# Quad 1 prepared inside the prologue, global scores in two column tiles, and top-k steps moved by one quad

## The chip, the cores and the metric

The kernel runs on one core of one Trainium2 chip. The core has a matrix engine (TensorE, PE in the profile), a vector engine (VectorE, DVE), an activation engine (ScalarE, ACT), GpSimd (POOL), and SyncE (SP), which here only issues transfers. The metric is the device time of one execution in microseconds. The kernel before takes 274.02 us, the median of three runs (272.31 to 275.62). Its profiled execution has a span of 268.8 us, and every moment named below is counted from the start of that span.

## The reference

Two stages follow one another: an attention with local and global tokens, and a layer of experts in which each expert takes at most 80 tokens.

```python
# attention: batch 8, heads 8, 512 local and 32 global tokens, head_dim 64
k_all = concat([k_g, k_l]); v_all = concat([v_g, v_l])
out_g = softmax(scale * q_g @ k_all.T) @ v_all          # global queries see every key
s_ll = where(|i - j| <= 32, scale * q_l @ k_l.T, -1e9)  # local queries: a band of keys
s_l  = concat([scale * q_l @ k_g.T, s_ll])              # ... and all global keys
out_l = softmax(s_l) @ concat([v_g, v_l])
x = concat([out_g, out_l]) as (4352 tokens, 512)

# experts: 8, w1 512x1024, w2 1024x512, capacity 80
logits = x @ w_gate; e = argmax(logits); gate = softmax(logits)[e]
for each expert: keep the 80 tokens with the largest gate
    out[tok] = gate * (relu(x[tok] @ w1[e]) @ w2[e])     # all other rows are 0
```

## The kernel before

A *quad* is four heads of one batch entry; there are 16 quads, numbered q. For each, queries and keys are loaded (`load_qk`), cast to fp16 and regrouped (`regroup`, into `qkr`), transposed on TensorE into `qkT` (`T_chunk`), and copied on GpSimd into a second arrangement (`kO_copy`, `kt_copy`). `L_fill` makes the local scores, `G_fill` the scores of local queries against global keys, `Q_fill` those of global queries. ScalarE takes the exponential of each out of PSUM. `G_all`, `H_chunk` and `Q_chunk` multiply by the values, `X_chunk` transposes the result for the gate logits. The steps `La` to `Ld` do the routing of one batch entry, two quads later; `some(n)` runs n pieces of the top-k work of a group of batch entries.

The global keys and queries stand in block-diagonal tiles, zeroed once:

```python
qbd = apool.tile([P, B, 4, 64], FP16, name="qbd")
kbd = apool.tile([P, B, 2, 320], FP16, name="kbd")
nc.gpsimd.memset(kbd[:], 0.0)
nc.gpsimd.memset(qbd[:], 0.0)

def G_fill(q):
    g_ps = psS([P, 512], FP32, f"G_ps{q}")          # pool "S": two PSUM buffers
    for j in range(2):
        nc.tensor.matmul(out=g_ps[:], lhsT=kbd[:, b, qd, 128 * j:128 * j + 128],
                         rhs=qkT[q % 2][:, j, 0:512], start=(j == 0), stop=(j == 1))
    nc.scalar.activation(out=s["eG"][:], in_=g_ps[:], func=AF.Exp, scale=scale)

def Q_fill(q, j):
    gq_ps = psS([P, NB, 64], FP32, f"gq_ps{q}_{j}")
    # ... five matmuls 128x64 with qbd, then the exponential

def L_fill(q, j):
    l_ps = [psS([P, 512], FP32, f"l_ps{q}_{j}_{hh}") for hh in range(2)]
    # ... one matmul of bandneg, 16 of 64x64, then two exponentials
```

The prologue and the first steps (cut):

```python
load_v(0)                      # v of quad 0, and vg of batch entry 0 in one transfer
load_qk(1)
regroup(0, 0)
regroup(0, 1, nc.vector.tensor_copy, nc.scalar.copy)
# ...
warm0(9)                       # matmuls that only keep TensorE busy
T_chunk(0, 0)
T_chunk(0, 1, (nc.vector.tensor_copy, nc.scalar.copy))
kO_copy(0, 0); kO_copy(0, 1); kt_copy(0)
setup_globals(0, 1, 1)         # fills kbd of batch entry 0
warm0(3)
# ... band
shift_v(0); L_fill(0, 0); mask(0, 0)
warm0(2)
setup_globals(0, 1, 0)         # fills qbd
L_fill(0, 1)
warm0(2)
G_fill(0)
for j in range(2):
    Q_fill(0, j)
regroup(1, 0, nc.vector.tensor_copy); mask(0, 1); regroup(1, 1, nc.vector.tensor_copy)
# ... loads
nc.gpsimd.memset(zt, 0.0); nc.gpsimd.memset(fin[:], 0.0)
for q in range(NQ):            # first = (q == 0)
    if late is not None and q == NQ - 1:
        Lc(late); some(2)
    G_all(q); H_chunk(q, 0)
    if first: T_chunk(1, 0)
    Q_chunk(q)
    if first: regroup(2, 0, ...); T_chunk(1, 1); kO_copy(1); kt_copy(1)
    elif q + 2 < NQ: T_chunk(q + 2, 0)
    if not first and q + 1 < NQ: L_fill(q + 1, 0); mask(q + 1, 0)
    # ... La, regroup(q + 3, 0), shift_v(q + 1)
    some(NS[q][0]); H_chunk(q, 1)
    if first: regroup(2, 1, ...); load_qk(4); L_fill(1, 0); mask(1, 0); shift_v(1)
    # ... Lb1
    some(NS[q][1])
    # ... L_fill(q + 1, 1), T_chunk(q + 2, 1), kO_copy, kt_copy when not first
    H_chunk(q, 2)
    # ... mask(q + 1, 1), Lm, Lb2; for the first: L_fill(1, 1), mask(1, 1), T_chunk(2, 0)
    G_fill(q + 1); Q_fill(q + 1, 0)
    H_chunk(q, 3)
    # ... for the first: T_chunk(2, 1), kO_copy(2), kt_copy(2)
    X_chunk(q, 0); Q_fill(q + 1, 1)
    # ... Lb3
    C_chunk(q); X_chunk(q, 1)
    some(NS[q][2])
```

`NS[14]` is `[1, 2, 1]`. After the loop come the rest of the routing, the zeroing of the output (17 transfers from `zt`), the global top-k, the gather of the kept tokens, eight experts and the scatter.

Of the kernel before, what the change touches and what calls it, by code (L numbers as in the profile page):

```python
# [18 lines left out]
P = 128  # L19
# [60 lines left out]
def kernel(  # L80
# [128 lines left out]
    def load_v(q):  # L209
# [6 lines left out]
        if qd == 0:  # L216
            nc.sync.dma_start(out=vg[b % 2][:, :, 0:64], in_=v_g[b].rearrange("(q f) g d -> (f g) q d", f=4))
# [11 lines left out]
    regroup(0, 0)  # L229
    regroup(0, 1, nc.vector.tensor_copy, nc.scalar.copy)  # L230
    load_qk(2)
    load_v(1)
    misc = const("misc", FP32)

# [22 lines left out]
    nc.vector.tensor_copy(out=identbf[:], in_=ident16[:])  # L257
# [7 lines left out]

    kbd = apool.tile([P, B, 2, 320], FP16, name="kbd")
    nc.gpsimd.memset(kbd[:], 0.0)
    nc.gpsimd.memset(qbd[:], 0.0)

    def setup_globals(b0, b1, *ts):  # L270
        for t, bd in ((1, kbd), (0, qbd)):
# [9 lines left out]
            for x, y, r, f in parts:  # L281
                if t == 1:
                    dst = kbd[x, b0:b1, r.start // 2, :].rearrange("x b (r c) -> x b r c", r=2)[
                        :, :, :, 64 * f:64 * f + 32]
                else:
                    dst = qbd[x, b0:b1, r, 32 * f:32 * f + 32]
                nc.vector.tensor_copy(out=dst, in_=src[y, :, :, f, :])
# [8 lines left out]
    for i in range(2):  # L296
        nc.vector.memset(Ls[i][:], 0.0)
    sc_all = cpool.tile([P, B, NB, E], FP32, name="sc_all")
# [32 lines left out]
    def G_fill(q):  # L331
# [4 lines left out]
        for j in range(2):  # L336
            nc.tensor.matmul(out=g_ps[:], lhsT=kbd[:, b, qd, 128 * j:128 * j + 128],  # L337
                             rhs=qkT[q % 2][:, j, 0:512], start=(j == 0), stop=(j == 1))
        nc.scalar.activation(out=s["eG"][:], in_=g_ps[:], func=AF.Exp, scale=scale)

    def Q_fill(q, j):
        b, qd = divmod(q, 2)
        gq_ps = psS([P, NB, 64], FP32, f"gq_ps{q}_{j}")
        for u in range(NB):
            k = qkT[q % 2][:, j, 512 + 128 * u:640 + 128 * u] if u < 4 else kbd[:, b, qd, 128 * j:128 * j + 128]
# [5 lines left out]
    def L_fill(q, j):  # L351
# [9 lines left out]
        for t in range(8) if q else (1, 2, 3, 4, 5, 6, 7, 0):  # L361
# [31 lines left out]
    def G_all(q):  # L393
# [5 lines left out]
        for u in range(4):  # L399
            for h in range(4):  # L400
                nc.tensor.matmul(out=s["o"][h][:, u, :],  # L401
                                 lhsT=s["eG"][32 * h:32 * h + 32, 128 * u:128 * u + 128],
                                 rhs=vg[b % 2][32 * h:32 * h + 32, qd, :], start=(u == 0), stop=False,
                                 skip_group_check=True)
# [21 lines left out]
    def Q_chunk(q):  # L426
# [4 lines left out]
        for u in range(NB):  # L431
            for h in range(4):
                f = slice(32 * (h // 2), 32 * (h // 2) + 32)
                x = slice(32 * h, 32 * h + 32)
                eQ = s["eQ"][h % 2]
                nc.tensor.matmul(out=og[x, :], lhsT=eQ[:, u, f] if u < 4 else eQ[x, u, f],  # L436
# [552 lines left out]
```

## Time and profile before

| what | value |
|---|---|
| time, median of 3 runs | 274.02 us (272.31 to 275.62) |
| span of the profiled execution | 268.8 us |
| TensorE busy | 230.1 us, 86% of the span |
| VectorE, ScalarE, GpSimd busy | 146.0, 136.6, 166.7 us |
| mean granted TensorE clock | 0.958 |
| first matmul of a quad's turn (G_all) of quads 0, 1, 2 | 15.14, 29.77, 40.60 us |
| the same of quads 14 and 15 | about 175.1, 187.6 us |
| first gather of tokens, first scatter | 228.31, 250.88 us |

"Busy" is the time in which an engine has an instruction in work. A releaser, written behind an arrow, is what ended the idle time before an instruction. The granted clock is the share of full TensorE speed in a stretch. The line numbers (L401) are those of the kernel before. The chain of work that ended last gives 42% of the span to TensorE, 19% to transfers and 15% to VectorE.

### The profile page before, as it was taken

The numbers are of one execution on the slowest core, as the hardware profiler recorded it, in microseconds if no ns is written. First come the engines' busy times: TensorE is split into PE (matmuls) and PEld (weight loads), VectorE is DVE, ScalarE is ACT, GpSimd is POOL, SyncE is SP. The second block draws the span as 40 slices with busy tenths as digits, with TensorE's granted clock in tenths as the row PEclk, the third lists the DMA queues.
The fourth block names the chain that finished last, engine by engine and source line by source line (L and its number), as shares of the span: only waits on it lengthen the run. The fifth ranks groups of instructions, "written<-read, shape, count | busy, mean of one in ns | idle before, by whom it ended". The sixth has DMA issues, their size and how long they took to land.

```text
span 268.8 us, 9537 instructions
## 1 busy us (share of the span) xinstructions
PE 230.1 (86%) x4022; PEld 159.4 (59%) x4022; DVE 146.0 (54%) x452; ACT 136.6 (51%) x237; POOL 166.7 (62%) x231
## 2 busy tenths in 40 slices
PE   6886979998899999998799999897986999399980
PEld 2365756776677577675657667665733445187750
DVE  2661661723753557776455955769687976012220
ACT  4455386776856759576486956835050000024420
POOL 9637776858859677784856878698362000790532
PEclk9798999999999999999999999999797999979995
DMA  7999879999999899899599969986999999999971
GB/s 231 303 278 202 265 134 222 196 221 193 241 218 248 169 220 255 162 265 264 130 230 235 234 116 184 183 151 126 182 296 262 235 233 307 408 413 239 214 221 50
DMA packets 67355, 60.05 MB, mean 223 GB/s; under 512 B 45808, under 2 KB 50160, under 8 KB 67312
## 3 DMA queue, kind: packets, MB, share of 16 engines
q1 hardware_dynamic: 59328, 40.61, 58.9%
q0 software_dynamic: 7840, 18.80, 37.7%
q8 instruction: 31, 0.51, 0.8%
q14 instruction: 12, 0.10, 0.1%
q10 hardware_dynamic: 144, 0.03, 0.1%
HBM read 61.57 MB, written 14.70 MB: 284 GB/s over the span
## 4 chain that ended last, share of the span: by engine, by line
PE 42%; DMA 19%; DVE 15%; issue 9%; ACT 7%; POOL 4%; SPq 1%; POOLq 1%; ACTq 0%; DVEq 0%
DMA out_dram<-zt 11%; PE o_ps L414 9%; DMA x_scr<-xgb 6%; PE o_ps L401 6%; PE T_ps L310 5%; PE og L436 5%; DVE xn L422 4%; ACT qkT L318 4%; PE x_ps L451 4%; PE lt_ps L473 3%; DVE scT L580 3%; PE l_ps L368 2%; DMA vb<-in_v_l_dram 2%; PE G_ps L337 2%; DVE lst L578 2%
## 5 line engine op out<-in xcount | busy, mean ns | idle before, releaser
L381 POOL TENSOR_TENSOR eL<-eL,band 128x512 f32<-128x512 f32 x30 | 37.9, 1265 | 34.6 <-ACT eL L373 34.6
L318 ACT COPY qkT<-T_ps 128x1024 f16<-128x1024 f16 x31 | 31.5, 1017 | 37.4 <-PE T_ps L310 37.4
L414 PE MATMUL o_ps<-vb,eL 128*64 128x65 f32 x1024 | 44.4, 230 | 0.0
L373 ACT ACTIVATE eL<-l_ps 128x512 f32<-128x512 f32 x64 | 34.8, 598 | 15.0 <-PE l_ps L368 14.8
L414 PEld LDWEIGHTS o_ps<-vb,eL 128*64 128x64 f32 x1024 | 35.7, 139 | 9.9 <-issue 6.0
L162 ACT CAST qkr<-qkb 128x1024 f16<-128x1024 f32 (+1 forms) x26 | 27.1, 1047 | 2.4 <-DMA qkb<-in_q_l_dram 2.0
L451 PE MATMUL x_ps<-misc,xn 128*128 128x128 f32 x128 | 20.5, 283 | 7.6 <-DVE xn L422 7.0
L649 PE MATMUL w_ps<-w1sb,onesb 128*128 128x512 bf16 x110 | 26.8, 398 | 0.0
L327 POOL COPY kO<-qkT 128x512 f16<-128x512 f16 x31 | 19.4, 650 | 11.0 <-ACT qkT L318 4.7
L927 ACT ACTIVATE fhT<-h_ps 128x320 bf16<-128x320 f32 x16 | 6.7, 431 | 36.4 <-PE h_ps L925 36.4
L903 POOL DMA_INDIRECT xg<-x_scr,idx x8 | 7.8, 971 | 27.2 <-DMA out_dram<-zt 25.0
L422 DVE TENSOR_TENSOR xn<-o_ps,rec 128x512 f32<-128x512 f32 x32 | 22.1, 692 | 2.4 <-POOL eL L381 0.5
L310 PE MATMUL T_ps<-ident,qkr 128*128 128x128 f16 x256 | 20.8, 227 | 2.8 <-DVE qkr L162 1.5
L421 DVE RECIPROCAL rec<-o_ps 128x8 f32<-128x8 f32 x32 | 6.5, 204 | 28.9 <-PE o_ps L414 28.7
L451 PEld LDWEIGHTS x_ps<-misc,xn 128*128 128x128 f32 x128 | 13.4, 140 | 10.2 <-PE gq_ps L346 6.3
L462 POOL CAST xb<-xn 128x1024 bf16<-128x1024 f32 x16 | 16.6, 1036 | 4.6 <-DVE xn L422 4.6
L649 PEld LDWEIGHTS <-onesb 128*128 128x128 bf16 x110 | 10.7, 102 | 13.9 <-issue 3.5
L310 PEld LDWEIGHTS <-qkr 128*128 128x128 f16 x256 | 15.2, 101 | 5.7 <-DVE qkr L162 1.6
L401 PE MATMUL o_ps<-vg,eG 32*128 32x65 f32 x512 | 18.4, 280 | 0.0
L441 DVE RECIPROCAL rg<-og 128x1 f32<-128x1 f32 x16 | 2.7, 169 | 28.1 <-PE og L436 28.1
L223 POOL COPY vb<-vb 64x1040 f32<-64x1040 f32 x16 | 17.1, 1067 | 0.9
L401 PEld LDWEIGHTS o_ps<-vg,eG 32*128 32x128 f32 x512 | 16.1, 190 | 2.3 <-issue 1.7
(156 smaller groups left out, 473.6 us busy)
## 6 DMA issues: line engine op xcount, KB each, us to landing
out_dram<-zt SPq DMA_DIRECT2D x17, 512.0 KB, 13.4
qkb<-in_q_l_dram SPq DMA_DIRECT2D x16, 512.0 KB, 5.2
qkb<-in_k_l_dram SPq DMA_DIRECT2D x16, 512.0 KB, 7.2
vb<-in_v_l_dram SPq DMA_DIRECT2D x16, 384.0 KB, 9.4
w2sb<-in_moe_w_dram POOLq DMA_DIRECT2D x12, 512.0 KB, 9.0
w1sb<-in_moe_w_dram POOLq DMA_DIRECT2D x10, 512.0 KB, 10.1
x_scr<-xb SPq DMA_DIRECT2D x8, 514.0 KB, 8.8
vb<-in_moe_w_dram POOLq DMA_DIRECT2D x6, 512.0 KB, 12.3
```

Of the source, the lines that this page charges most:

```text
L162: cp(out=qkr[q][:, t, i].rearrange("p i g d -> p g i d"), in_=qkb[q % 2][:, t, :, i])
L223: nc.gpsimd.tensor_copy(out=v[64:128, 17:33], in_=v[64:128, 0:16])
L310: nc.tensor.transpose(out=T_ps[:, i].rearrange("x a p -> x (a p)"), in_=qkr[q][:, t, i].rearrange("p g d -> p (g d)"), identity=ident16[:, :])
L318: nc.scalar.copy(out=dst, in_=src)
L327: (nc.gpsimd if q or a else nc.vector).tensor_copy(out=kO[q % 2][:, a], in_=qkT[q % 2][:, a, 576:1088].rearrange("x (u w y) -> x u w y", w ...
L373: nc.scalar.activation(out=eL[:], in_=l_ps[hh][:], func=AF.Exp, scale=scale)
L381: eng.tensor_tensor(out=eL[:], in0=eL[:], in1=band[:].rearrange("p t i -> p (t i)"), op=ALU.mult)
L401: nc.tensor.matmul(out=s["o"][h][:, u, :], lhsT=s["eG"][32 * h:32 * h + 32, 128 * u:128 * u + 128], rhs=vg[b % 2][32 * h:32 * h + 32, qd, ...
L414: nc.tensor.matmul(out=o[64 * odd:64 * odd + 64, u, :], lhsT=s["eL"][h][:, 64 * t:64 * t + 64], rhs=v[:, 17 * odd + 4 * h + u, :], start=F ...
L422: nc.vector.tensor_tensor(out=s["xn"][:, :, 64 * h - 64:64 * h + 64].rearrange("p u (h d) -> p h u d", h=2), in0=o2[:, :, :, 0:64], in1=re ...
L451: nc.tensor.transpose(out=x_ps[:, 128 * u:128 * u + 128], in_=s["xn"][:, u, 128 * j:128 * j + 128], identity=identf[:, :])
L649: nc.tensor.matmul(out=w_ps[:], lhsT=onesb[:], rhs=w1sb[0][:, 0, 0:512], start=True, stop=True)
```

## The change

It has five parts.

1. Quad 1 is cast between the first local scores of quad 0 and the copies that fill `qbd`, and its transposes and GpSimd copies are done before the loop, between the query scores of quad 0. Step 0 of the loop then starts with quad 1 ready and takes the same order as the others. The masks of quad 0 stand behind the casts.
2. The memset of `kbd` goes to VectorE, those of `kbd` and `qbd` run over 4-byte words, and those of `zt` and `fin` go from the prologue into step 0. `kbd` shrinks from 5120 to 2048 fp16 columns.
3. `G_fill` writes its two halves into partitions 0 to 63 and 64 to 127 by two matmuls of 64 columns, where it accumulated two of 128. The heads then stand in the order 0, 2, 1, 3, so `vg` is loaded by four transfers of 32 partitions each where it was one.
4. One top-k step less runs in the middle of step 14 and one less at its end; step 15 starts with four where it had two.
5. Five warm matmuls stand ahead of the last transposes of step 14; three warm matmuls of the prologue are gone.

```diff
-            nc.sync.dma_start(out=vg[b % 2][:, :, 0:64], in_=v_g[b].rearrange("(q f) g d -> (f g) q d", f=4))
+            for r in range(4):
+                h = 2 * (r % 2) + r // 2
+                nc.sync.dma_start(out=vg[b % 2][32 * r:32 * r + 32, :, 0:64],
+                                  in_=v_g[b].rearrange("(q f) g d -> f g q d", f=4)[h])
...
-    kbd = apool.tile([P, B, 2, 320], FP16, name="kbd")
-    nc.gpsimd.memset(kbd[:], 0.0)
-    nc.gpsimd.memset(qbd[:], 0.0)
+    kbd = apool.tile([P, B, 4, 64], FP16, name="kbd")
+    nc.vector.memset(kbd[:].rearrange("p b r c -> p (b r c)").bitcast(FP32), 0.0)
+    nc.gpsimd.memset(qbd[:].rearrange("p b r c -> p (b r c)").bitcast(FP32), 0.0)
...
-            nc.tensor.matmul(out=g_ps[:], lhsT=kbd[:, b, qd, 128 * j:128 * j + 128],
-                             rhs=qkT[q % 2][:, j, 0:512], start=(j == 0), stop=(j == 1))
+            nc.tensor.matmul(out=g_ps[64 * j:64 * j + 64, :], lhsT=kbd[:, b, 2 * qd + j, :],
+                             rhs=qkT[q % 2][:, j, 0:512], start=True, stop=True)
...
-        for t in range(8) if q else (1, 2, 3, 4, 5, 6, 7, 0):
+        for t in range(8) if q > 1 else (1, 2, 3, 4, 5, 6, 7, 0):
...
-    NS = [...] [1, 1, 0], [2, 2, 3], [1, 2, 1], [0, 0, 0]]
+    NS = [...] [1, 1, 0], [2, 2, 3], [1, 1, 0], [0, 0, 0]]
...
+    kt_copy(0)
     kO_copy(0, 1)
-    kt_copy(0)
     setup_globals(0, 1, 1)
-    warm0(3)
+    warm0(2)
     ... band
     shift_v(0)
     L_fill(0, 0)
-    mask(0, 0)
+    regroup(1, 0, nc.vector.tensor_copy)
     warm0(2)
     setup_globals(0, 1, 0)
     L_fill(0, 1)
-    warm0(2)
-    G_fill(0)
-    for j in range(2):
-        Q_fill(0, j)
-    regroup(1, 0, nc.vector.tensor_copy)
-    mask(0, 1)
     regroup(1, 1, nc.vector.tensor_copy)
     ... loads
-    nc.gpsimd.memset(zt, 0.0)
-    nc.gpsimd.memset(fin[:], 0.0)
+    warm0(1)
+    G_fill(0)
+    for j in range(2):
+        Q_fill(0, j)
+        T_chunk(1, j)
+    for j in range(2):
+        mask(0, j)
+    kO_copy(1, 0)
+    kt_copy(1)
+    kO_copy(1, 1)
...
             Lc(late)
-            some(2)
+            some(4)
...
-        if first:
-            T_chunk(1, 0)
         Q_chunk(q)
         if first:
             regroup(2, 0, nc.vector.tensor_copy)
-            T_chunk(1, 1)
-            kO_copy(1)
-            kt_copy(1)
...
         if first:
             regroup(2, 1, nc.vector.tensor_copy)
             load_qk(4)
-            L_fill(1, 0)
-            mask(1, 0)
-            shift_v(1)
+            nc.gpsimd.memset(zt, 0.0)
+            nc.gpsimd.memset(fin[:], 0.0)
...
         C_chunk(q)
+        if q == NQ - 2:
+            warm(5)
         X_chunk(q, 1)
```

## The prediction

> **What bounds the kernel now.** I read the page's busy rows first, then windows cut at the first global-value matmul of each quad (the 32 matmuls of line 401 that open a quad's turn), then the order of instructions in the places that stood out. The windows (columns: stretch, its length, then busy us of TensorE, weight load, VectorE, ScalarE, GpSimd, the granted clock, the DMA share, GB/s):
>
> ```profile
> 0.00:15.14 15.14, 10.64 (x80) 4.78 (x80) 7.19 (x28) 7.50 (x11) 12.36 (x20) 0.89 1.00 275
> 15.14:29.77 14.63, 11.68 (x229) 9.16 (x226) 6.39 (x14) 7.76 (x13) 8.13 (x10) 0.88 1.06 243
> ...
> 107.00:119.13 12.13, 11.14 (x233) 8.06 (x231) 9.76 (x33) 8.42 (x15) 9.28 (x14) 1.00 0.96 216
> ...
> 165.27:175.16 9.89, 9.22 (x212) 7.09 (x211) 6.52 (x22) 6.39 (x11) 7.77 (x12) 1.00 1.02 170
> 175.16:187.60 12.44, 10.36 (x216) 7.26 (x216) 9.95 (x34) 5.90 (x12) 10.97 (x16) 1.00 0.76 143
> 187.60:195.00 7.40, 6.90 (x147) 5.84 (x147) 4.75 (x16) 0.00 (x0) 3.14 (x6) 0.77 0.92 167
> ```
>
> A settled quad takes 9.9 us (even step, no routing work) or about 12 us (odd), and TensorE is busy for all but 0.7 to 1.0 us of it: the loop is bound by TensorE. Two places are worse. Step 0 takes 14.63 us with 2.95 us idle and clock 0.88; step 14 takes 12.44 us, although an even step costs 9.9 and this one has no transposes of a later quad. The change aims at exactly these. After 195 us the routing, the gather and the expert layers follow in a chain that starts from the last quad, and the zeroing of the output (13.4 us to landing, first issue at 193.78) is issued behind it, so I take the tail as moving with the end of the loop.
>
> The waits of step 0, from the order of instructions (start, duration, what, idle before and releaser):
>
> ```profile
> 5.54 1.79 POOL L268 MEMSET qbd<- 128x2048 f16 x1
> 5.90 1.72 DVE L162 CAST qkr<-qkb 128x512 f16<-128x512 f32 x1 [4.52 <-DMA qkb<-in_k_l_dram]
> 20.25 1.62 POOL L327 COPY kO<-qkT 128x512 f16<-128x512 f16 x2 [4.37 <-ACT qkT L318]
> 21.83 0.23 POOL L322 COPY qkT<-qkT 128x64 f16<-128x64 f16 x1
> 22.11 0.20 PE L368 MATMUL l_ps<-qkT 64*128 64x64 f16 x2 [2.03 <-POOL qkT L322]
> ```
>
> The cast at 5.90 ends at 7.62, right after GpSimd's memset ends at 7.33, while ScalarE's half of the same size takes 0.62. And quad 1's local scores start only at 22.11: its casts, transposes and GpSimd copies all lie inside step 0.
>
> The clock over stretches of 3.4 us (same columns as above):
>
> ```profile
> 20.85:24.25 3.40, 2.07 (x54) 1.53 (x54) 0.56 (x1) 1.23 (x3) 1.73 (x4) 1.00 0.77 161
> 24.25:27.65 3.40, 3.40 (x37) 2.59 (x34) 0.44 (x2) 2.68 (x5) 3.28 (x5) 0.50 1.13 202
> 184.70:188.10 3.40, 1.53 (x30) 1.07 (x26) 3.19 (x13) 1.51 (x3) 2.44 (x5) 1.00 0.33 60
> 188.10:191.50 3.40, 3.40 (x80) 2.82 (x73) 1.22 (x5) 0.00 (x0) 1.84 (x4) 0.50 0.92 196
> ```
>
> [...]
>
> [...] In the trace the 32 matmuls of `og`, 32 columns each, and the 8 behind them take 0.84 us together[...]; no 64-column pair of 512 elements is in this trace. [...] here GpSimd takes 0.94 us for 1024 fp32 and 1.79 us for 2048 fp16[...].
>
> **The start: memsets, early quad 1.** The memsets leave GpSimd by about 2.2 us, so VectorE's cast of quad 0's keys should take some 0.3 us instead of 1.72, and the second transpose chunk starts near 6.6 instead of 7.68. That lead is then spent on a new wait: the query scores of quad 0 now need `qbd`, whose copies stand behind the cast of quad 1's queries. Counting 2 KB packets, quad 1's queries finish moving at about 10.5 us and its keys at 11.9, and quad 0 shows some 0.8 us from the last packet to the cast. The three extra `vg` issues (0.49 us each, ahead of quad 1's load at 6.69) delay it by 0.6 to 1.4. So: queries cast from 12.0, `qbd` ready at 13.6, keys cast by 14.3, second transpose of quad 1 until 15.0. The loop starts at about 15.1, as before.
>
> But step 0 is then shorter. Gone are 16 transposes (2 x 0.6 us) and the 2.0 us wait at 22.11. Following TensorE in order at full clock: G_all 1.05, H 0.62, Q 0.84, scores of quad 1 from 17.5, their second half bounded by ScalarE's exponentials until 19.9, then H, T, G, T, X and the wait for ScalarE's `qkT` copy, to an end at about 24.8. Before it was 29.77: 5.0 us. From this I take off about 1.0, since the start now has TensorE idle for some 2 us between 11 and 13.6 and a half-clock stretch can land on step 0 (up to 1.7). GpSimd also holds the next step: masks, `shift_v`, two memsets and `kO` put quad 2's `kt` copy at about 27.9, against a need at 24.8 + 3.1 = 27.9. **4.0 us**, between 2.5 and 5.
>
> **Global scores in two column tiles.** Two matmuls of 128x512 that accumulate become two of 64 columns side by side. The pair now occupies 0.44 us (from 126.98 to 127.42, below), so 0.22 saved per quad. In even steps it is hidden:
>
> ```profile
> 126.26 1.10 ACT L373 ACTIVATE eL<-l_ps 128x512 f32<-128x512 f32 x2
> 126.98 0.61 PE L337 MATMUL G_ps<-qkT,kbd 128*128 128x512 f16 x2
> 127.42 0.28 PE L346 MATMUL gq_ps<-qbd,qkT 128*128 128x64 f16 x4
> ```
>
> `gq_ps` needs the second PSUM buffer of the pool with two, which ScalarE frees at 127.36, 0.06 before `gq_ps` begins. In odd steps it is free earlier (140.16, where the pair starts at 140.14). So 7 odd steps x 0.21 + 7 even x 0.05 = 1.8; I count **1.6 us**.
>
> **Top-k steps and warm matmuls.** One removed step is 0.37 + 0.08 + 0.35 = 0.8 us of VectorE. In step 14 one of the two between `L` and `lmax` goes, and the one at the end goes:
>
> ```profile
> 183.39 1.32 DVE L504 TENSOR_TENSOR oh<-L,lmax 128x40 f32<-128x40 f32 x1
> ...
> 186.12 0.66 PE L451 MATMUL x_ps<-misc,xn 128*128 128x128 f32 x4 [1.28 <-DVE xn L422]
> ```
>
> The second x_ps of step 14 waits 1.28 us for `xn`, whose VectorE queue is late by these steps and by `oh`, which takes 1.32 instead of 0.19 beside GpSimd's mask (183.39, 1.26). Taking 0.8 out, and some of the collision, readies `xn` near 185.0; but five warm matmuls of 0.21 us now stand before x_ps, so it starts near 186.0 either way. Ahead of the next G_all stand `sc_all` and its transpose, earlier by 0.7. Then the warm matmuls should keep the clock up: G_all 1.48, H 1.06, og 1.40 at half clock against 1.05, 0.62, 0.84 at full, 1.43 us. VectorE's four steps at the start of step 15 (3.3 us) then outlast TensorE by 0.4 and more and give some of it back. 0.7 + 1.0 = **1.7 us**, or 0.7 if the clock still drops.
>
> **The sum.** 4.0 + 1.6 + 1.7 = 7.3 us; I take 7.0, since a tail with DMA share near 1.0 may not follow in full. 274.0 - 7.0 = 267.0.
>
> **Rivals.** (a) The wait only moves: quad 1's load comes too late through `vg`'s issues, the loop starts at 16 to 16.5 and runs step 0 at half clock. For it speaks the in-order queue at 6.16; against it that no transposes are left in step 0. Start gain 2, total near 269. (b) The tail holds: zeroing and weights keep the DMA busy, the first scatter (250.88, after 8.96 us of issue wait) does not come earlier, and the end moves by half. For it: DMA share 1.0 after 195. Against: the zeros are issued only after the last quads. About 270.5. (c) No half-clock stretch in either place, and the saved G time also frees even steps: 10 us, 264.
>
> **Range and chances.** The three parts vary between 2.5 and 5, 0.8 and 2.6, 0.7 and 2.3: 4.0 to 9.9. With the spread of the runs (272.31 to 275.62) 263.5 to 270.8. 2% is 268.5, 1.5 above my centre: 0.66 faster, 0.31 the same, 0.03 slower.
>
> **What would show it.** Right: the cast of quad 0's keys near 0.3 us; G_all of quad 0 near 15.1 and of quad 1 at 25 to 26.5; no idle of 2 us before quad 1's scores; the pair of G_ps at about 0.22 us up to the next matmul; odd steps 0.2 shorter and even ones unchanged; o_ps of quad 15 at 1.05 us; the first gather about 7 us earlier. Wrong: quad 1's casts after 14 us, half clock inside step 0 or 15, a G_ps pair that still takes 0.44, or a first scatter still near 251.

## The result, and the profile after

| | before | after |
|---|---|---|
| time, median of 4 runs each, side by side | 273.24 us (272.31 to 275.62) | 265.01 us (264.58 to 266.47) |
| span of the profiled execution | 268.8 us | 263.2 us |
| mean granted TensorE clock | 0.958 | 0.968 |
| VectorE, ScalarE, GpSimd busy | 146.0, 136.6, 166.7 us | 151.2, 135.8, 160.9 us |
| first matmul of quad 0, 1, 2 | 15.14, 29.70, 40.53 us | 15.91, 27.52, 38.81 us |
| first matmul of quad 14, 15 | 175.09, 187.57 us | 170.46, 182.77 us |
| last transpose (x_ps) of quad 15 | 194.28 us | 188.32 us |
| first gather, first scatter | 228.31, 250.88 us | 222.25, 245.56 us |

The ratio is 0.9696, interval 0.9619 to 0.9773. A second comparison on another chip, with 20 runs of the kernel after and 39 of the kernel before, gave 0.9902 (0.9858 to 0.9946). (A ratio leaves disturbed runs out, so it is not the quotient of the medians.) Both lie below 1, but only the first is clear of a difference of 2%. They don't agree on how much, and the question of where the time went has to answer that too.

The two spans differ by 5.6 us. The lead of the kernel after can be followed quad by quad, as the difference of the moments at which `G_all` starts (29.70 and 40.53 for quads 1 and 2 of the kernel before, 0.07 earlier than the times given ahead of the prediction):

| stretch | lead gained in it, us | what it is |
|---|---|---|
| until quad 0 | -0.77 | the loop starts later |
| step 0 | +2.95 | 14.56 became 11.61 |
| step 1 | -0.46 | 10.83 became 11.29: TensorE waits 0.88 for the `kt` copy of quad 2 |
| steps 2, 8, 10, 12, 13 | +1.42 | 0.28 or 0.29 each |
| steps 3, 5, 6, 7, 11 | +0.11 | -0.11 to +0.07 each |
| step 4 | -0.41 | 12.30 became 12.71; the same kernel takes 12.30 in another execution |
| step 9 | +1.79 | 12.25 became 10.46: two stalls of the kernel before, see the first experiment |
| step 14 | +0.17 | 12.48 became 12.31 |
| step 15 to its last x_ps | +1.16 | 6.71 became 5.55 |
| sum | 5.96 | the lead at the last x_ps, 194.28 - 188.32 |

The windows of the kernel after (columns: stretch, its length, then busy us of TensorE, weight load, VectorE, ScalarE and GpSimd with their instructions, the granted clock, the DMA share, GB/s):

```profile
0.00:15.91 15.91, 10.45 (x95) 5.63 (x95) 8.24 (x31) 8.68 (x13) 5.87 (x17) 0.94 0.89 250
15.91:27.52 11.61, 10.95 (x208) 8.57 (x207) 5.74 (x11) 6.59 (x11) 6.28 (x8) 0.78 1.08 231
...
170.46:182.77 12.31, 11.51 (x219) 7.96 (x218) 9.35 (x31) 5.85 (x12) 11.31 (x17) 1.00 0.91 171
182.77:190.00 7.23, 6.24 (x152) 4.96 (x155) 6.60 (x23) 0.59 (x1) 4.13 (x8) 1.00 0.92 166
10.70:14.10 3.40, 1.13 (x18) 0.62 (x12) 1.95 (x5) 1.68 (x3) 2.75 (x3) 1.00 0.95 290
14.10:17.50 3.40, 3.40 (x54) 3.20 (x51) 1.96 (x4) 2.69 (x4) 0.23 (x1) 0.50 1.16 315
17.50:20.90 3.40, 3.40 (x69) 2.38 (x67) 0.44 (x3) 0.00 (x0) 1.11 (x3) 0.50 1.19 227
```

The windows of 3.40 us lie ahead of and behind the change of the granted clock at 14.12, from where the trace has half clock for 6.83 us and then full clock for 177.49.

GpSimd's work before the loop fell from 12.36 to 5.87 us. Step 0 has 208 matmul records where it had 229, and only 0.66 us of idle where it had 2.95, but its clock is 0.78: the stretch from 10.70 has TensorE busy for 1.13 of 3.40 us, and the two stretches after it run at half clock. The stretch from 182.77 shows clock 1.00, where the kernel before had 0.77.

The order of instructions in the prologue (start, duration, what, idle before and its releaser):

```profile
1.24 0.95 POOL L265 MEMSET qbd<- 128x1024 f32 x1
1.54 0.91 DVE L264 MEMSET kbd<- 128x1024 f32 x1 [0.16 <-issue]
6.22 0.43 DVE L162 CAST qkr<-qkb 128x512 f16<-128x512 f32 x1 [2.50 <-DMA qkb<-in_k_l_dram]
6.40 1.90 SPq L219 DMA_DIRECT2D vg<-in_v_g_dram  x4
8.34 0.43 SPq L153 DMA_DIRECT2D qkb<-in_q_l_dram  x1
12.06 1.26 DVE L162 CAST qkr<-qkb 128x1024 f16<-128x1024 f32 x1 [2.25 <-DMA qkb<-in_q_l_dram]
13.35 0.81 DVE L279 COPY qbd<-g_ps 64x64 f16<-64x64 f16 x4
13.79 0.29 PE L342 MATMUL gq_ps<-qbd,qkT 128*128 128x64 f16 x4 [1.90 <-DVE qbd L279]
15.91 1.99 PE L398 MATMUL o_ps<-vg,eG 32*128 32x65 f32 x32
```

The memsets are over by 2.45 us and the cast of quad 0's keys takes 0.43 us where it took 1.72. Then the wait that had been inside step 0 stands ahead of the loop: SyncE spends 1.90 us on the four `vg` issues before it can issue quad 1's queries, VectorE waits 2.25 us for them, the `qbd` copies stand behind that cast, and TensorE waits 1.90 us for `qbd`. The first `G_all` takes 1.99 us, at half clock.

In step 10 the two kernels agree to 0.01 us until the scores of local queries against global keys; from there the order of instructions shows the column tiles. Kernel before, whose step starts at 131.31, then kernel after, whose step starts at 127.59:

```profile
140.14 0.60 PE L337 MATMUL G_ps<-qkT,kbd 128*128 128x512 f16 x2
140.58 0.28 PE L346 MATMUL gq_ps<-qbd,qkT 128*128 128x64 f16 x4
```

```profile
136.32 0.39 PE L330 MATMUL G_ps<-qkT,kbd 128*64 128x512 f16 x2
136.64 0.29 PE L342 MATMUL gq_ps<-qbd,qkT 128*128 128x64 f16 x4
```

Counted from the start of the step, the pair begins at 8.83 and 8.73, and the matmuls behind it at 9.27 and 9.05. The 128x64 form follows a group of the same form (`o_ps`, 128*64), and starts 0.10 earlier; the pair itself takes 0.44 and 0.32 to the next matmul. Together this is 0.22, and the step ends 0.28 earlier.

The end of step 14 and step 15 in the kernel after, in the order of instructions:

```profile
178.65 0.18 DVE L502 TENSOR_TENSOR oh<-L,lmax 128x40 f32<-128x40 f32 x1
...
179.10 1.26 POOL L377 TENSOR_TENSOR eL<-eL,band 128x512 f32<-128x512 f32 x1
179.26 1.16 DVE L509 SCALAR_TENSOR_TENSOR oh<-cs,oh 128x40 f32<-128x40 f32 x1
...
181.46 0.60 PE L449 MATMUL x_ps<-misc,xn 128*128 128x128 f32 x4
...
182.57 0.27 PE L549 MATMUL t_ps<-misc,sc_all 128*40 128x128 f32 x1 [0.51 <-DVE xb L531]
182.77 1.12 PE L398 MATMUL o_ps<-vg,eG 32*128 32x65 f32 x32
```

The first `oh`, 1.32 us before, takes 0.18: it ends before GpSimd's mask starts. The second one, 0.20 us before, now stands beside that mask and takes 1.16. The collision moved by two instructions. `G_all` of quad 15 takes 1.12 us where it took 1.55.

### The profile page after: what moved, and what is told of

Its sections match the earlier page's. It is cut to its first block, busy times and chain, and to the rows that moved or that the text cites. A ratio compares the mean times of both kernels' runs of the same rounds, so it can differ in the third digit from the quotient of the medians.

```text
span 263.2 us, 9558 instructions
## 1 busy us (share of the span) xinstructions
PE 227.9 (87%) x4025; PEld 157.9 (60%) x4025; DVE 151.2 (57%) x453; ACT 135.8 (52%) x237; POOL 160.9 (61%) x230
## 4 chain that ended last, share of the span: by engine, by line
PE 51%; DVE 15%; issue 8%; ACT 8%; DMA 8%; POOL 6%; SPq 3%; POOLq 1%; ACTq 0%; DVEq 0%
PE o_ps L411 8%; PE w_ps L647 7%; PE o_ps L398 5%; DVE xn L419 5%; PE T_ps L303 4%; PE y_ps L930 4%; PE og L434 4%; ACT qkT L311 4%; PE h_ps L923 4%; PE x_ps L449 3%; DMA out_dram<-zt 3%; PE lt_ps L471 3%; DMA xg<-x_scr,idx 2%; DVE scT L578 2%; ACT eL L369 2%
## 5 line engine op out<-in xcount | busy, mean ns | idle before, releaser
L647 PE MATMUL w_ps<-w1sb,onesb 128*128 128x512 bf16 x115 | 27.8, 395 | 0.0
L320 POOL COPY kO<-qkT 128x512 f16<-128x512 f16 x31 | 18.6, 624 | 7.8 <-ACT eg L515 4.1
L398 PE MATMUL o_ps<-vg,eG 32*128 32x65 f32 x512 | 19.1, 285 | 0.0
L398 PEld LDWEIGHTS o_ps<-vg,eG 32*128 32x128 f32 x512 | 16.8, 194 | 2.5 <-issue 1.7
L225 POOL COPY vb<-vb 64x1040 f32<-64x1040 f32 x16 | 17.2, 1073 | 1.1 <-DMA vb<-in_v_l_dram 1.1
L226 POOL COPY vb<-vb 64x1040 f32<-64x1040 f32 x16 | 17.1, 1067 | 0.9
```

The source lines that it names most:

```text
L225: nc.gpsimd.tensor_copy(out=v[0:64, 17:33], in_=v[0:64, 1:17])
L320: (nc.gpsimd if q or a else nc.vector).tensor_copy(out=kO[q % 2][:, a], in_=qkT[q % 2][:, a, 576:1088].rearrange("x (u w y) -> x u w y", w ...
L398: nc.tensor.matmul(out=s["o"][h][:, u, :], lhsT=s["eG"][32 * r:32 * r + 32, 128 * u:128 * u + 128], rhs=vg[b % 2][32 * r:32 * r + 32, qd, ...
L647: nc.tensor.matmul(out=w_ps[:], lhsT=onesb[:], rhs=w1sb[0][:, 0, 0:512], start=True, stop=True)
```

## The experiments

The theory after this reading: half-clock stretches and waits in the prologue set what the start is worth; the column tiles are worth 0.28 us in long steps and little in short ones; the five warm matmuls keep the clock up in step 15; and the rest of the 8.2 us between the medians is time that belongs to single executions. Rivals give the parts other shares. The runs stand in three groups, each on its own chip with its own runs of the kernel before: 271.56 us (267.85 to 276.60) in the first, 275.19 (270.60 to 282.35) in the second, 274.06 (273.35 to 275.90) in the third. Step lengths are read from one profiled execution of each kernel.

**The kernel before, unchanged, once more.** Step 9 of the first trace held a gap of TensorE in the middle of a group, with no semaphore event to end it (order of instructions):

```profile
130.63 0.20 PE L346 MATMUL gq_ps<-qbd,qkT 128*128 128x64 f16 x1 [1.57 <-issue]
```

> The kernel before, unchanged, for a second trace. Theory: the 1.57 us and 0.85 us in which TensorE of step 9 (119 to 131 us) waits for nothing that the profile shows belong to one execution, not to the kernel, so step 9 is near 10.1 us here and about 2 us turn up elsewhere or not at all. Rival: they come with this program's layout, and step 9 takes 12.2 us again.

One execution, 276.03 us. Step 9 takes 9.91 us, where it took 12.25. Steps 2, 4, 7 and 8 repeat to 0.01 us (11.91, 12.29, 10.06, 12.01). But other steps are now longer, step 5 by 3.9 us:

```profile
86.26 0.45 PE L414 MATMUL o_ps<-vb,eL 128*64 128x65 f32 x7 [2.13 <-issue]
```

From 87.25 the clock is at half for 6.83 us, and step 6 takes 14.15 us where it took 12.24. So the 1.79 us of step 9 need not come from the change: whether TensorE stalls at such a place, and for how long, belongs to the execution. Most steps without a stall can be compared between two traces to 0.1 us, and spans can't be compared to better than some microseconds.

**The new start alone**: the order of the prologue and of step 0, and the memsets (with `kbd` in its old size, now on VectorE). `G_fill` and the end are as before.

```diff
-    nc.gpsimd.memset(kbd[:], 0.0)
-    nc.gpsimd.memset(qbd[:], 0.0)
+    nc.vector.memset(kbd[:].rearrange("p b r c -> p (b r c)").bitcast(FP32), 0.0)
+    nc.gpsimd.memset(qbd[:].rearrange("p b r c -> p (b r c)").bitcast(FP32), 0.0)
...
-    mask(0, 0)
+    regroup(1, 0, nc.vector.tensor_copy)
...
+    for j in range(2):
+        Q_fill(0, j)
+        T_chunk(1, j)
...
-        if first: T_chunk(1, 0)
```

> The kernel before with the early quad 1, the new memsets and the new places of the masks alone: accumulated 128-column scores, one transfer for vg, old top-k steps, no warm matmuls in step 14. Theory A (the start brings what the trace of the changed kernel shows, less the delay by vg's transfers): G_all of quad 1 near 26.8 us (before 29.7, changed 27.5), with a half-clock stretch of 6.8 us inside step 0 again; time about 2.9 us less than before, ratio 0.989. Theory B (without the three extra vg transfers quad 1 lands early enough that no half clock falls into step 0): G_all of quad 1 near 25 us, time 4.7 less, ratio 0.983.

Median 270.59 us (21 runs), ratio 0.9908 (0.9856 to 0.9960). Order of instructions of its prologue:

```profile
11.24 1.41 DVE L162 CAST qkr<-qkb 128x1024 f16<-128x1024 f32 x1 [1.78 <-DMA qkb<-in_q_l_dram]
13.12 0.29 PE L341 MATMUL gq_ps<-qbd,qkT 128*128 128x64 f16 x4 [0.45 <-DVE qbd L281]
14.82 1.12 PE L396 MATMUL o_ps<-vg,eG 32*128 32x65 f32 x32
```

Without the extra `vg` issues quad 1's queries are cast 0.82 us earlier, TensorE waits 0.45 us where it waited 1.90, step 0 runs at full clock in 9.96 us, and quad 1 starts at 24.78: 4.9 us ahead of the kernel before. The median shows only half of that. Its trace has 6.1 us of stalls, the longest 2.77 us at 151.76, where the first trace of the kernel before has 2.8; whether the lead is lost to them on average, or the prologue runs otherwise in other executions, one trace can't tell.

**The column tiles alone**, with the four `vg` transfers and the small `kbd`:

```diff
-    kbd = apool.tile([P, B, 2, 320], FP16, name="kbd")
+    kbd = apool.tile([P, B, 4, 64], FP16, name="kbd")
...
-            nc.tensor.matmul(out=g_ps[:], lhsT=kbd[:, b, qd, 128 * j:128 * j + 128],
-                             rhs=qkT[q % 2][:, j, 0:512], start=(j == 0), stop=(j == 1))
+            nc.tensor.matmul(out=g_ps[64 * j:64 * j + 64, :], lhsT=kbd[:, b, 2 * qd + j, :],
+                             rhs=qkT[q % 2][:, j, 0:512], start=True, stop=True)
```

> The kernel before with the two column tiles for the global scores alone, with the four vg transfers and the smaller kbd that they need. Theory A: 0.22 us in steps with routing, none in the others (the second PSUM buffer of the pool is freed by ScalarE only then): 1.6 us less, ratio 0.994. Rival B: all steps gain 0.22, 3.3 us, ratio 0.988. Rival C: the extra transfers delay quad 1 and eat it: ratio 1.00.

Median 268.55 us (20 runs), ratio 0.9868 (0.9823 to 0.9912), some 3.6 us. In the loop it is what the theory says: steps 2, 8 and 12 are 0.27 to 0.29 shorter (11.64, 11.73, 11.63), step 6 is 0.40 shorter, steps 3, 4, 5, 11 and 13 between 0.01 and 0.08, some 1.5 us over the steps without a stall. The rest is at a place that nobody had named. Order of instructions in the prologue:

```profile
2.98 1.79 POOL L271 MEMSET qbd<- 128x2048 f16 x1
5.87 0.43 DVE L162 CAST qkr<-qkb 128x512 f16<-128x512 f32 x1 [4.49 <-DMA qkb<-in_k_l_dram]
13.22 1.12 PE L403 MATMUL o_ps<-vg,eG 32*128 32x65 f32 x32
```

The memset of the smaller `kbd` ends so early that GpSimd is done at 4.77, before VectorE's cast starts. The cast takes 0.43 us instead of 1.72, and the loop starts at 13.22 instead of 15.14 (14.72 to 15.78 in the traces with the old start and the old `kbd`). Quad 1 starts at 27.32: 2.4 us of lead at the place where the whole change has 2.2.

**The end alone**: one top-k step fewer in the middle and one at the end of step 14, four ahead of step 15, five warm matmuls.

```diff
-            some(2)
+            some(4)
...
-  [1, 2, 1],
+  [1, 1, 0],
...
         C_chunk(q)
+        if q == NQ - 2:
+            warm(5)
         X_chunk(q, 1)
```

> The kernel before with the moved top-k steps and the five warm matmuls of step 14 alone. Theory A: step 14 hardly shorter (0.2 us), step 15 at full clock, the second x_ps of quad 15 about 1.3 us earlier than in the kernel before: 1.3 us less, ratio 0.995. Rival B: the end of the loop is followed by a fixed tail and nothing arrives: 1.00.

Median 269.38 us (20 runs), ratio 0.9966 (0.9933 to 0.9999). Its `G_all` of quad 15 takes 1.12 us and the last x_ps starts 5.56 us after it, where the kernel before has 6.71. Step 14 takes 13.02 us with a stall of 0.63 inside it, so no gain can be read there. In this trace the end is worth 1.15 us in step 15; by the runs it is 0.9 us (0.0 to 1.8).

**The kernel after, unchanged, on the second chip**: 20 runs beside 39.

> The changed kernel, unchanged, timed and traced again. Theory: the loop's own shape repeats (G_all of quad 1 at 27 to 28, if the half clock falls into step 0 again, 25 if not), and the rest of the spread comes from stalls of TensorE at other places than in the first trace. Ratio to the kernel before 0.972 to 0.978, as its many runs have a median of 271.6.

Median 270.75 us (267.78 to 275.71), ratio 0.9902. The ratio of 0.972 to 0.978 that was expected did not come. The half clock comes at the same place again (14.76, for 6.83 us), and quad 1 starts at 27.72, as expected. Step 0 takes 12.79 us with a stall of 0.60 in it, where it took 11.61; steps 2, 3, 5, 7 and 8 repeat to 0.12 us, and step 4 takes 12.30. Later traces with the same prologue do not all repeat the start (see the run with the old top-k steps). The expert stage, from its first transpose to the end of its last matmul, takes 31.4 us, where it took 26.8 in the first trace.

**`vg` behind quad 1's load**, in the kernel after:

```diff
-    load_v(0)          # with the four vg transfers
-    load_qk(1)
+    load_v(0)          # v alone
+    load_qk(1)
+    load_vg(0)         # the four vg transfers
```

> The changed kernel with the first four vg transfers issued behind quad 1's queries and keys instead of ahead of them. Theory A (the transfers delay quad 1 by 0.8 us, and this lengthens TensorE's gap enough for the half clock): quad 1's queries are cast at about 11.3 us instead of 12.06, G_all of quad 0 at 14.9, and no half-clock stretch in step 0: G_all of quad 1 near 25, 2.5 us less than the changed kernel. Rival B (the half clock comes from the gap before it, whatever vg does): cast at 11.3, but G_all of quad 1 at 26.7, 0.8 less.

Median 267.34 us (4 runs), ratio 0.9819 (0.9739 to 0.9899). Order of instructions:

```profile
11.22 0.69 DVE L162 CAST qkr<-qkb 128x1024 f16<-128x1024 f32 x1 [1.48 <-DMA qkb<-in_q_l_dram]
...
14.10 1.12 PE L403 MATMUL o_ps<-vg,eG 32*128 32x65 f32 x32
...
20.32 0.20 PE L369 MATMUL l_ps<-qkT 64*128 64x64 f16 x1 [1.54 <-issue]
```

The cast starts 0.84 us earlier and the loop 1.81 us earlier, at full clock. Then a stall of 1.54 us falls into step 0, a half-clock stretch (3.4 us) follows at 20.64, and quad 1 starts at 26.75, 0.77 us ahead of the kernel after. This is the number of rival B, but not its reason: the four issues do delay quad 1, and the half clock at 14 us goes with that delay. The time does not separate the two kernels, as their intervals overlap.

**Nine warm matmuls in the gap**, in the kernel after, and nothing moved:

```diff
     G_fill(0)
+    warm0(9)
     for j in range(2):
         Q_fill(0, j)
```

> The changed kernel with nine warm matmuls behind the first global scores, in the gap in which TensorE waits for qbd. Theory A (the half clock of step 0 comes from that gap): no half-clock stretch between 14 and 21 us, G_all of quad 1 near 25.2 instead of 27.5, 2.3 us less. Rival B (ScalarE's and GpSimd's work sets step 0 and not TensorE's clock): G_all of quad 1 stays within 0.5 us of 27.5.

Median 270.78 us (20 runs), ratio 0.9857 (0.9822 to 0.9891). Its windows over the stretches of its own clock at the same place:

```profile
10.37:13.77 3.40, 3.03 (x28) 1.36 (x27) 1.48 (x4) 2.65 (x5) 2.85 (x3) 1.00 1.02 346
13.78:17.18 3.40, 3.40 (x66) 2.64 (x65) 2.19 (x5) 2.07 (x4) 0.00 (x0) 1.00 1.12 305
```

The loop starts at 16.04, 0.13 later than in the kernel after, since the transfers are what they were. But step 0 is at full clock: 10.33 us, with a stall of 0.85 in it, where the kernel after has 11.61. So it was the idle time ahead of `gq_ps` that cost the clock, and the clock cost step 0 some 2 us (11.61 - 10.33 + 0.85 = 2.1). In the time this does not show beyond the intervals (0.9857 beside 0.9902).

**The kernel after without the five warm matmuls:**

```diff
         C_chunk(q)
-        if q == NQ - 2:
-            warm(5)
         X_chunk(q, 1)
```

> The changed kernel without the five warm matmuls of step 14. Theory A (they keep the clock up): a half-clock stretch falls on step 15, its o_ps take 1.5 us, and the time is 1 us longer. Rival B (the earlier xn alone suffices, the warm matmuls only stand in the way): G_all of quad 15 about 0.5 us earlier at full clock, time 0.5 us less.

Median 268.09 us (5 runs), ratio 0.9854 (0.9814 to 0.9894). Half clock returns at 188.08, for 3.4 us, and the last x_ps starts at 193.64 after a `G_all` at 186.92: 6.72 us, where the kernel after has 5.55 and the kernel before 6.71.

```profile
188.09:191.49 3.40, 3.40 (x76) 2.94 (x78) 2.42 (x9) 0.00 (x0) 1.20 (x3) 0.50 1.01 207
```

The 1.16 us in step 15 of this trace are the clock's alone. Step 14 takes 12.06 us. The time is not 1 us longer, as theory A had it: 0.9854 beside 0.9902, with intervals that overlap.

**The kernel after with the top-k steps where they had been**, the warm matmuls kept:

```diff
-  [1, 1, 0],
+  [1, 2, 1],
...
-            some(4)
+            some(2)
```

> The changed kernel with the top-k steps where they were (1, 2, 1 in step 14 and two at the start of step 15), the five warm matmuls kept. Theory A (the steps hold xn of step 14): oh of step 14 again 1.3 us beside GpSimd's mask, the wait for xn fills the warm matmuls, G_all(15) comes 12.5 to 13 us after G_all(14) instead of 12.0 to 12.3, and in step 15 the x_ps come up to 0.5 us sooner, since two steps less stand ahead of them: 0.3 to 0.5 us longer in all. Rival B (nothing in VectorE's order matters there): both distances within 0.1 us of the changed kernel.

One execution, 272.64 us. Step 14 takes 13.11 us, against 11.88 to 12.31 in the kernel after and its other variants. The collision is back where it was (order of instructions):

```profile
182.36 1.32 DVE L502 TENSOR_TENSOR oh<-L,lmax 128x40 f32<-128x40 f32 x1
...
186.53 1.12 PE L398 MATMUL o_ps<-vg,eG 32*128 32x65 f32 x32
```

Step 15 is 0.27 us shorter (5.29), with two top-k steps fewer at its head. Moving the steps thus gives 0.5 to 1.0 us, once the warm matmuls stand there; against the kernel before, which has neither, step 14 gains only 0.2 to 0.6.

This trace also shows how little a single start says. Its prologue and step 0 are those of the kernel after, but `gq_ps` waits only 0.54 us for `qbd`, the clock is full from 11.48 to 21.72, and then TensorE stalls in step 0:

```profile
23.00 0.23 PE L364 MATMUL l_ps<-qkT 64*128 64x64 f16 x1 [2.81 <-issue]
```

The clock is at half for 6.83 us from 21.72, step 0 takes 14.71 us, and quad 1 starts at 30.22, later than in the first trace of the kernel before.

**Warm matmuls ahead of the experts.** TensorE idles before the experts' first transposes, for 3.91 us in the first trace of the kernel before and 4.16 in that of the kernel after, and there half clock follows for 3.41 us, from 235.88 and from 229.16.

```diff
     load_w(NRES + 4, (0, 1, 2, 3))
-    warm(16)
+    warm(34)
```

> The changed kernel with 34 warm matmuls instead of 16 behind the one-hot matmuls, so that TensorE stays busy until the first gathered tokens land. Theory A (the 4.2 us gap before the first xT_ps starts the half-clock stretch at the experts, 3.4 us long in one trace of the changed kernel and 13.65 in the other): no half clock from the first xT_ps on; the last y_ps comes 1.7 to 6 us earlier after the first gather than in the two traces of the changed kernel; time 2 to 3 us less in the median. Rival B (the scatters wait for the zeroing, and the experts' clock is hidden): no half clock, but the time within 1 us of the changed kernel.

Median 270.18 us (4 runs), ratio 0.9818 (0.9732 to 0.9904). The idle time is gone, and behind the first transposes of the experts the half clock comes only at 240.36, for 3.4 us. But the expert stage still takes 30.2 us, and the interval overlaps with those of the kernel after. Neither theory had foreseen what it waits for instead, 3.2 us for a VectorE copy that itself shows no releaser on the core. It is seen best in the next run.

**A version from these findings**: quad 1's load ahead of quad 0's values, the memsets of `zt` and `fin` in step 3, and the 34 warm matmuls.

```diff
-    load_v(0)
-    load_qk(1)
+    load_qk(1)
+    load_v(0)
...
-            nc.gpsimd.memset(zt, 0.0); nc.gpsimd.memset(fin[:], 0.0)   # in step 0
+        if q == 3:
+            nc.gpsimd.memset(zt, 0.0); nc.gpsimd.memset(fin[:], 0.0)
...
-    warm(16)
+    warm(34)
```

> Changed kernel with quad 1's load ahead of the values of quad 0, the memsets of zt and fin in step 3 instead of 0, and 34 warm matmuls before the experts. Theory A (quad 1's landing set the start): queries of quad 1 cast near 9.5 us, G_all of quad 0 near 13.5 and of quad 1 near 23.5 to 24, no half clock in step 0, no wait for the kt copy in step 1; with the experts at full clock 5 to 6 us less than the changed kernel. Rival B (the values then land too late, and GpSimd's shift_v holds H_chunk of quad 0): G_all of quad 1 at 26 or later.

Median 269.37 us (4 runs), ratio 0.9803 (0.9735 to 0.9872). The start does what it should: loop at 14.40, no half clock in step 0 (10.61 us), quad 1 at 25.01, 2.5 us ahead of the kernel after. It is not the expected 23.5 to 24: at 16.57 TensorE waits 1.05 us for GpSimd's `shift_v`, the wait that rival B named. Moving the memsets does not help: GpSimd's `kt` copy is early now, but TensorE waits 0.79 us for a VectorE cast instead, then 0.48 for an exponential, and step 1 takes 11.62 us. Stalls of 2.02 us at 86.12 and 0.77 us at 120.20 and a long expert stage (31.1 us) follow. It isn't shown to be better than the kernel after, since its interval overlaps with both of that kernel's. What holds the expert stage, in the order of instructions of this kernel and then of the kernel after:

```profile
234.55 0.77 ACT L926 ACTIVATE fhT<-h_ps 128x320 bf16<-128x320 f32 x2 [38.08 <-remote]
234.71 0.32 DVE L916 COPY fxT<-xT_ps 128x320 bf16<-128x320 bf16 x1 [4.06 <-remote]
235.04 1.43 PE L924 MATMUL h_ps<-fxT,w1sb 128*128 128x80 bf16 x32 [3.21 <-DVE fxT L916]
```

```profile
230.90 0.44 ACT L925 ACTIVATE fhT<-h_ps 128x320 bf16<-128x320 f32 x1 [34.96 <-PE h_ps L923]
```

In the kernel after ScalarE takes the first expert's result as soon as TensorE has it. In the other, ScalarE and VectorE both begin again some 4 us later, within 0.2 us of each other, with nothing on the core that releases them.

**The kernel before a third time**, on the third chip.

> The kernel before once more, for the stalls of TensorE and the length of the half-clock stretch at the experts. Theory: stalls of 1 to 5 us in all, at other steps than in its two other traces, each ending some 1.4 us behind a transfer on the instruction queue; steps without a stall repeat to 0.1 us.

One execution, 277.29 us. Steps 2, 3, 4, 5 and 7 repeat (11.91, 9.90, 12.30, 10.11, 10.19). But the stalls are not at other steps: step 9 takes 12.95 us, with 1.68 us at 124.43 and 0.68 at 132.77, ahead of the same two instructions as in the first trace.

```profile
124.43 0.34 PE L436 MATMUL og<-vb,eQ 128*32 128x65 f32 x7 [1.68 <-issue]
```

The 14 traces together say where TensorE can stall. Count its records (matmuls, weight loads and semaphore instructions) in the order in which they start. All 47 gaps of the loop of 0.35 us or more without a releaser then stand behind 193 to 195 such records plus a multiple of 256, and each ends 1.3 to 1.9 us after one of the 31 or 32 transfers of 16 KB on the queue that the page names `q8 instruction`. In the first trace the gaps of 0.41, 0.85 and 1.57 us stand behind 3009, 4289 and 4545 records, and end 1.42, 1.61 and 1.41 us after such a transfer; in the kernel after, those of 0.57 and 0.42 us stand behind 3009 and 4289, and end 1.50 and 1.38 us after one. So the places repeat from trace to trace, and whether TensorE stalls there, and for how long, varies. In step 6 a stall is there in 10 of the 14 traces, in step 9 at the `og` above in 9. What TensorE waits for at these places was not shown: no run moved them.

The first such place lies in step 0. With the old start TensorE comes there just after its wait of 2.03 us for GpSimd, 2.3 to 4.0 us after the end of the transfer (in the first trace at 22.62 and 18.92), and stalls in none of five traces. With the new start, which has no such wait, it goes on from there 1.3 to 2.0 us after the transfer, and in six of nine traces it has stalled there, for 0.5 to 2.8 us.

The expert stage takes 31.7 us, where the two earlier traces of this kernel have 26.7 and 26.0. All traces of the first group and the two first ones have 26.0 to 27.6 us, all of the second and third group 30.0 to 31.9. On the third chip this holds for the kernel before too, so the long expert stage is not the change's there; the second group has no trace of the kernel before.

## Why the prediction was right

The total was predicted at 267.0 us and came out at 265.0, inside the range; the direction was right. The steps behind it were partly right. That the size came so close is in part luck, as the sum at the end shows.

**The start, predicted 4.0, measured 2.2 at quad 1** (and 0.5 of that is given back in step 1). The chain of waits was foreseen as it came: queries cast from 12.0 (12.06), second transposes of quad 0 near 6.6 (6.71), no idle before quad 1's scores, `vg`'s issues costing 0.6 to 1.4 (0.84). `qbd` was ready at 14.16, not 13.6, as the cast of the queries took 1.26 us, and the loop started at 15.91, not 15.1. "Following TensorE in order at full clock" was right: 24.8 - 15.1 is 9.7 us for step 0, and at full clock it takes 9.96 in the run with the new start alone and, less its stall, 9.5 in the one with nine warm matmuls. The step that failed is the allowance "I take off about 1.0 ... a half-clock stretch can land on step 0 (up to 1.7)". The idle time of 1.9 us brought two stretches, and they cost 2.1 us, 1.1 more than allowed. Together with the late start of 0.8, this is about the missing 1.8. For the start, rival (a) is what happened: loop at 16, step 0 at half clock, gain 2; its counter-argument, that no transposes are left in step 0, overlooked those of quad 2. (The prologue lost two warm matmuls, from 16 to 14, and not the three named among the parts of the change.)

This is the first pair of traces. Four more have the same prologue and step 0 as the kernel after, and step 0 takes 11.61 to 14.71 us in the five. Two of them have no half clock at 14 us, but stall for 1.66 and 2.81 us in step 0 and run the next 6.83 us at half clock. Quad 2 starts at 38.58 to 40.99 us in the five, and at 39.76 to 41.99 in the four traces with the old start and the old `kbd`. The means, 39.6 and 40.7, differ by 1.1 us, where the first pair has 1.7. The stall in step 0 was on no list of costs.

One more thing was misplaced. The faster cast of quad 0's keys (0.43 us, where some 0.3 was the author's estimate) was put down to the memsets leaving GpSimd, and its gain called "spent on a new wait". It takes 1.72 us beside a memset and 0.43 where the memsets are over; why was not shown. The small `kbd` is enough for the fast cast, and the run that has it without the new start begins the loop 1.9 us earlier. The new start, which casts quad 1 ahead of `qbd`, then takes this back.

**The column tiles, predicted 1.6, measured 1.5** over steps 2 to 13 (the two rows of the table), and about the same alone. That two tiles side by side take half of the pair's 0.44 us was the author's estimate. What was measured in step 10 fits it in size, half from the pair (0.32 where it was 0.44) and half from its earlier start (0.10): 0.22 us at the pair where nothing hides it, next to nothing where ScalarE frees the PSUM buffer late. In step 9 of the kernel after, 0.49 us pass from the pair (124.53) to the matmuls behind it (125.02), where it was 0.44, and ScalarE's exponentials end at 124.97, 0.05 ahead of those. Not every long step gains: 4 gains nothing, and no run shows why. Step 6 gains 0.07 with a stall in both traces, and 0.22 between two traces without one (12.06 and 11.84). The short step 13 gains 0.29. The names were the wrong way round: the long steps with routing are the even ones. From this also followed "an even step costs 9.9", said of step 14; its measure is 11.9, so it was 0.6 us too long, not 2.5.

**The end, predicted 1.7, measured 1.3 in the first pair, about 1.0 over all traces.** "1.43 us" for full clock in step 15, less what VectorE's four steps give back, was put at 1.0; the trace has 1.16, and without the warm matmuls nothing of it. "x_ps starts near 186.0 either way", 10.9 us into step 14, came as 11.0. The 0.7 that `sc_all` was to gain is 0.17 here and 0.4 to 0.6 in the other traces with the whole change: the first `oh` is clear of the mask, and a later instruction on as many elements stands beside it instead. That second `oh` takes 1.16 us and ends 0.06 us after the mask of 1.26, where it took 0.20 us from 185.02 in the kernel before, 0.37 behind the mask's end. Why it takes longer beside the mask was not shown.

The half clock in step 15 was taken as given, and it is not. Without the five warm matmuls it falls on step 15 in three of six traces. In the other three the last x_ps comes 5.28 or 5.29 us after `G_all`, 0.27 sooner than with the whole change. In the third trace of the kernel before, the second x_ps of step 14 waits 1.28 us for `xn` as in the first; but the boundaries of its clock stretches lie elsewhere, and no stretch there is as empty as the 1.53 us from 184.70 in the first:

```profile
186.03:189.43 3.40, 2.12 (x34) 1.69 (x33) 3.23 (x10) 2.12 (x6) 2.36 (x5) 1.00 0.75 146
189.44:192.84 3.40, 2.81 (x85) 2.27 (x83) 2.86 (x10) 0.59 (x1) 3.40 (x6) 1.00 0.44 120
```

So the warm matmuls save 1.16 us in step 15 when the half clock would have come and nothing when it would not; the top-k steps moved to its head cost 0.27 either way. The mean over the six traces is 6.20 us, in those with the whole end it is 5.56: 0.6 less.

**The tail follows.** The lead is 5.96 us at the last x_ps, 6.06 at the gather, 5.3 at the scatter and 5.6 at the end. Rival (b), a tail held by the zeroing, falls for this pair.

**The sum.** What the first pair of traces gives to the change is 2.2 - 0.5 + 1.5 + 0.2 + 1.2 = 4.6 us, not 7.3. With the means over all traces it is 1.1 for the start with step 1, 1.5, about 0.4 for step 14 and 0.6 for step 15: 3.6 us, a rough figure from few executions on several chips. The second comparison's ratio is, on its 275.19 us, 2.7 us (1.5 to 3.9), which holds 3.6; the first one's, on 273.24, is 8.3 us (6.2 to 10.4), more than either sum. So the predicted 7.0 came close to 8.2 because the four and four runs of the first comparison differ by more than the change's own part. The stalls of TensorE make up 1 to 6 us in each trace, and within 7 us behind 11 of the 17 over 1.3 us a group of 16 `o_ps` takes 0.9 to 1.1 us, where it takes 0.69 at full clock; what else sets the first four and four runs apart stays open, as does what holds ScalarE and VectorE in the expert stage.

## What to carry to other kernels

A wait that is moved off one path can cost more than its length: in the kernel after, TensorE was busy for 1.13 us of one stretch of 3.4, and the next 6.83 us ran at half speed. Fill the gap or order the loads so that it does not arise, and size this by whole stretches, with a chance that it does not come at all. A wait can also hide another: when the wait of 2.03 us for GpSimd in step 0 went, a stall of TensorE without a releaser came into view there, of 0.5 to 2.8 us in six of nine traces. Before work is reordered around a slow instruction, ask what slows it; here a memset of 2048 columns in place of 5120 was over before VectorE's cast, which took 0.43 us instead of 1.72, and brought at the first quads, in its one trace, what the whole reordering did. And compare steps, not spans, and more than one trace: most steps without a stall agree to 0.1 us between two executions, while the times of one kernel spread over 10 us and one step 0 over 3.

## What the runs showed of the hardware

- In the clock records of the first traces of both kernels the granted clock is full or half. It stays at half for 3.41 or 6.83 us and at full for 3.41, 10.24, 13.65, 23.89, 27.31, 160.43 or 177.49 us, all within 0.01 us of multiples of 3.413 (the last stretch, which the end of the trace cuts, left out). Full-clock stretches of 3.4 us between these moments with TensorE busy for 1.31 us or less were all followed by half clock, and those with 2.38 or more by none. Between the two both occur: in the kernel before 1.44, 1.53 and 2.07 us (from 201.76, 184.70 and 20.85) were followed by it and another 1.44 us (from 229.06) was not, in the kernel after 1.83 and 2.10 us (from 3.88 and 222.34) were not, and in the run with the column tiles alone 2.22 us (from 126.83) was. In the kernel after half clock lasted 6.83 us behind the 1.13 us from 10.70, and 3.41 us behind 0.67 and 0.32 us (from 195.03 and 225.75).
- In step 10 two 512-column matmuls in tiles of 64 columns, behind a group of the same tile form, take 0.32 us to the next matmul and start 0.10 us earlier, against 0.44 for two that accumulate over the full width.
- Two VectorE operations on 128x40 elements take longer beside a GpSimd multiply of 1.26 us: the first `oh` 1.32 us beside it in the kernel before and 0.18 ahead of it in the kernel after, the second `oh` 1.16 us beside it in the kernel after and 0.20 behind it in the kernel before. Starting the first one 0.45 us ahead of the multiply, and no longer together with it, only changed which one was hit.
- TensorE stalls in the middle of a group without a releaser, for up to 2.8 us. In 14 traces all 47 such gaps of 0.35 us or more in the loop lie a multiple of 256 of TensorE's records apart (to within 2), 1.3 to 1.9 us behind the end of a 16 KB transfer on the queue `q8 instruction`; which of the places stalls differs between executions of one kernel.
